# Memory products of a segmented attention in three PSUM banks instead of two

## The chip, the core and the metric

The kernel runs on one core of a Trainium2 chip. The metric is device time in microseconds for one execution; the figure of a kernel is the median of its runs. The profile shows one execution, instruction by instruction, on the core's engines: TensorE (PE, with its weight loads as PEld), VectorE (DVE), ScalarE (ACT), GpSimd (POOL) and the queue that issues most DMAs (SP).

## What is computed

Two independent results stand side by side in the output. One is a Fourier mixing of `B_x` by dense products. The other is a segmented attention over 2048 rows in four segments of 512, with 32 heads of 18 features, in which each segment also reads a memory of the segments before it:

```python
for s in range(N):
    qs, ks, vs = q[:, :, s], k[:, :, s], v[:, :, s]
    logits = jnp.einsum("bhqd,bhkd->bhqk", qs, ks) * scale + mask
    p = _softmax(logits, axis=-1)
    a_dot = jnp.einsum("bhqk,bhkd->bhqd", p, vs)
    pq = phi(qs)
    num = jnp.einsum("bhld,bhde->bhle", pq, M)
    den = jnp.einsum("bhld,bhd->bhl", pq, z)[..., None] + 1e-6
    a_mem = num / den
    o = g * a_mem + (1.0 - g) * a_dot
    outs.append(o)
    pk = phi(ks)
    M = M + jnp.einsum("bhld,bhle->bhde", pk, vs)
    z = z + jnp.einsum("bhld->bhd", pk)
```

The change concerns `num` and `den`, the products of `pq` with the memory.

## The kernel before

**Stages.** The first 220 us project q, k and v, build the memory and read it, segment by segment (loop at L495). The rest interleaves attention with the dense products of the Fourier part, by a list of steps with fixed weights, and ends with the output projection. The order on each engine is the order in which the program is written (manual schedule, L45); nothing is reordered. `later(n, ...)` puts a call n ticks later in that order.

**A segment.** After the nine q and k projections (`project_qk`, from L258) comes the memory stage: four blocks of 128 rows, `project_v(s, j, ...)` (L304), called blocks 0 to 3 here. In a block TensorE makes the two halves of v, 16 heads each, v0 and v1, with 14 matmuls of 288 columns each (L82). ACT copies each half out of PSUM as bf16 (L319) and, in segments 0 to 2, as fp32r (L59); DVE subtracts that copy from it (L60) and writes the remainder `vr` (L322), which is the last read of the PSUM tile. After v0, segments 0 to 2 transpose k (`k_natural`, tiles `kt`, L300), and ACT and DVE make phi of k from it (L214 to L218, POOL L219). After each half the next part of `lookup` runs (L325). From block 1 on, segments 0 to 2 end a block with `accumulate` for the block before (L358), which adds to the memory sums in three further PSUM tiles. In segment 3, DVE has the splitting of the Fourier weights (L122 to L125) and of the first chunks (L451, L453) in its queue instead. SP's queue holds the loads, the copies between DRAM tensors and, among them, the store of each lookup's result `am`.

**A lookup** (L385 to L414; segments 1 to 3, so 12 in all) multiplies pq by the memory. The features lie in five chunks of 128, 128, 128, 128 and 64 rows, with 7, 7, 7, 7 and 4 heads of their own; a window of 8 heads of 19 columns (18 features and z) is taken for each chunk, and the eighth head is shared with the next chunk. Everything is in two parts, high and low, of fp32r: `pq_hi`, `pq_lo`, `md[:, c, 0]` and `md[:, c, 1]`, and of the four products low times low is left out.

- The first half, before v1: chunks one to three, three matmuls of 152 columns each, added up in one PSUM tile `o` (L388 to L391); ACT copies 21 heads into `nd` (L392).
- The second half, after v1: chunk four in a second tile `u`, `pq_hi` against both halves of the memory in one matmul of 304 columns, which leaves two results side by side, and `pq_lo` against the high half (152); chunk five with one matmul of 152 columns for both halves of 4 heads (L397 to L399). ACT copies (L400, L401); DVE adds what is shared or lies beside it (L402 to L405), adds 1e-6, takes the reciprocal and multiplies by the gate (L408 to L410); POOL multiplies (L412), and the result is stored.

The sums in `den` are held in the second tile's last 32 columns, so that this tile is free only after w (L410).

**PSUM.** v0, v1, kt, the q and k projections and the lookup's tiles share a ring of five tiles of one bank each, tag "acc" (`bufs=5`). A new tile waits for the last reader of the tile whose bank it gets. TensorE executes in order, so that a matmul that waits for a bank holds up all that follows it.

Of the kernel before, what the change touches and what calls it, by code (L numbers as in the profile page):

```python
# [12 lines left out]
F32 = mybir.dt.float32  # L13
# [3 lines left out]
AF = mybir.ActivationFunctionType  # L17
OP = mybir.AluOpType
# [4 lines left out]
S, D, H, DH, NSEG, L = 2048, 576, 32, 18, 4, 512  # L23
P = 128
# [16 lines left out]
def infini_attention_and_fnet(ctx: ExitStack, tc: tile.TileContext, xT, wqk, w8, wv, wo, beta, xtT, cT, hT, out):  # L41
    nc = tc.nc
    act, dve, pool, pe = nc.scalar, nc.vector, nc.gpsimd, nc.tensor
# [42 lines left out]
    def later(n, fn, *a):  # L86
        due.setdefault(clock[0] + n, []).append((fn, a))
# [10 lines left out]
    ps = p1.enter_context(tc.tile_pool(name="ps1", bufs=2, space=PSUM))  # L98
# [93 lines left out]
    pq_hi = sb.tile([P, 5, L], F32R, name="pq_hi")  # L192

    pq_lo = sb.tile([P, 4, L], F32R, name="pq_lo")
# [13 lines left out]
    md = sb.tile([P, 5, 2, 8, 19], F32R, name="md")  # L208
# [152 lines left out]
    def memory():  # L361
# [20 lines left out]
            dve.tensor_tensor(md[:64, 4, 1], mf[:64, 4], md[:64, 4, 0].bitcast(F32), OP.subtract)  # L382
        later(4, cut)

    def lookup(s, j):  # L385
        js = slice(j * P, (j + 1) * P)
        nd = sb.tile([P, H, 19], F32, name="nd", bufs=2)
        o = ps.tile([P, 3, 8, 19], F32, name="look", tag="acc", bufs=5)  # L388
        for c in range(3):
            for n, (a, half) in enumerate(((pq_hi, 1), (pq_hi, 0), (pq_lo, 0))):  # L390
                pe.matmul(o[:, c], a[:, c, js], md[:, c, half], start=c + n == 0, stop=True, skip_group_check=True)  # L391
        act.activation(nd[:, :21].rearrange("p (c h) e -> p c h e", c=3), o[:, :, :7], AF.Copy)  # L392
        yield

        u = ps.tile([P, L], F32, name="look", tag="acc", bufs=5)
        u3, u4 = (u[:, at:at + 2 * n].rearrange("p (k h e) -> p k h e", k=2, e=19) for at, n in ((0, 152), (304, 76)))
        pe.matmul(u3, pq_hi[:, 3, js], md[:, 3], start=True, stop=True, skip_group_check=True)  # L397
        pe.matmul(u3[:, 0], pq_lo[:, 3, js], md[:, 3, 0], start=False, stop=True, skip_group_check=True)
        pe.matmul(u4, pq_hi[:, 4, js], md[:, 4, :, 4:], start=False, stop=True, skip_group_check=True)  # L399
        act.activation(nd[:, 21:28], u3[:, 0, :7], AF.Copy)  # L400
        act.activation(nd[:, 28:], u4[:, 0], AF.Copy)  # L401
        dve.tensor_tensor(nd[:, 7:22:7], nd[:, 7:22:7], o[:, :, 7], OP.add)  # L402
        dve.tensor_tensor(nd[:, 28:], nd[:, 28:], u4[:, 1], OP.add)
        dve.tensor_tensor(nd[:, 28], nd[:, 28], u3[:, 0, 7], OP.add)
        dve.tensor_tensor(nd[:, 21:29], nd[:, 21:29], u3[:, 1], OP.add)  # L405
        w = sb.tile([P, H, 1], F32, name="w", bufs=2)
        den = u[:, 456:456 + H, None]
        dve.tensor_scalar(den, nd[:, :, DH:], 1e-6, None, op0=OP.add)  # L408
        dve.reciprocal(den, den)
        dve.tensor_tensor(w, den, g[:, :, None], OP.mult)  # L410
        am = sb.tile([P, H, DH], F32, name="am", tag="p", bufs=5)
        pool.tensor_tensor(am, nd[:, :, :DH], w.to_broadcast([P, H, DH]), OP.mult)  # L412
        later(1, dma, amd[s][j], am.rearrange("p h d -> p (h d)"))
        yield  # L414
# [16 lines left out]
    def c_load(n):  # L431
        if n < len(CHUNKS) and n not in c_seen:
            c_seen.add(n)
            src, at, k = CHUNKS[n]
            t = sr.tile([P, 5, P], F32, name="craw", bufs=4)
            dma(t[:, :k], src[at])
            c_raw[n] = t
# [57 lines left out]
    for s in range(NSEG):  # L495
# [32 lines left out]
        for j in range(4):  # L528
            project_v(s, j, lookup(s, j) if s else iter(()))
            tick()  # L530
            for k in ((0, 1), (2, 3), (4,), ())[j] if s == 0 else ():
                load_x(1, k)
            if more and j in (1, 2):
                split_x(s + 1, j - 1)
            if not more and j == 1:
                stacks(sr, 1)
            if not more and j == 2:
                attention_constants()
            if not more and j == 0:
                h_split(0, 2)  # L540
                h_split(0, 3)
            if not more and j == 1:
                h_split(0, 4)
                c_cut(0, dve)
                c_cut(1, dve)
            if not more and j in (1, 3):
                c_load(3 + j // 2)
            if more and j:
                accumulate(j - 1)
# [4 lines left out]
    ps = ctx.enter_context(tc.tile_pool(name="ps2", bufs=2, space=PSUM, reuse_waits="tile"))  # L554
# [49 lines left out]
    def chunk(n):  # L604
        c_load(n + 4)
        return c_split.pop(n)
# [393 lines left out]
    for t in range(NT):  # L1000
# [3 lines left out]
        for h in range(2):  # L1004
            cs = slice(h * 288, h * 288 + 288)
            o = ps.tile([P, 288], F32, name="d", bufs=3)
# [53 lines left out]
```

## Time and profile before

| | us |
|---|---|
| runs | 999.23, 999.67, 1004.48 |
| median | 999.67 |
| profiled execution | 1000.37 |
| its span, from the first to the last instruction | 998.6 |
| mean granted TensorE clock | 0.999 |

The profile's page gives each engine's busy time and its share of the span, and the chain of work that ended last, followed back from the last instruction. In a timeline each row is the start in us, the duration, the engine, the line of the code, the operation, its output and inputs with their shapes, how many instructions are merged into the row (x2), and in brackets how long the engine was idle before it and what released it. [...] In a table by stretch, each row is a stretch of the span with its length and the busy time of each engine.

### The profile page before, as it was taken

The numbers are of one execution on the slowest core, as the hardware profiler recorded it, in microseconds if no ns is written. First come the engines' busy times: TensorE is split into PE (matmuls) and PEld (weight loads), VectorE is DVE, ScalarE is ACT, GpSimd is POOL, SyncE is SP. The second block draws the span as 40 slices with busy tenths as digits, with TensorE's granted clock in tenths as the row PEclk, the third lists the DMA queues.
The fourth block names the chain that finished last, engine by engine and source line by source line (L and its number), as shares of the span: only waits on it lengthen the run. The fifth ranks groups of instructions, "written<-read, shape, count | busy, mean of one in ns | idle before, by whom it ended". The sixth has DMA issues, their size and how long they took to land.

```text
span 998.6 us, 25575 instructions
## 1 busy us (share of the span) xinstructions
PE 989.0 (99%) x9291; PEld 923.7 (93%) x9291; DVE 753.9 (75%) x2048; ACT 710.9 (71%) x1677; POOL 635.5 (64%) x700
## 2 busy tenths in 40 slices
PE   9999999999999999999999999999999999999998
PEld 7988989898999999999999999999999999999998
DVE  6657668594678777878898888898888899998321
ACT  6667576663887877878788788877767777777243
POOL 2657576686767667666766777776767767767000
PEclk9999999999999999999999999999999999999999
DMA  7447556787578898899999887789999999899555
GB/s 254 161 131 231 205 177 238 236 306 214 138 169 204 208 230 210 209 229 217 254 228 247 220 208 198 181 197 223 223 239 214 242 237 243 228 202 189 137 152 138
DMA packets 305182, 208.92 MB, mean 209 GB/s; under 512 B 206240, under 2 KB 259872, under 8 KB 305056
## 3 DMA queue, kind: packets, MB, share of 16 engines
q1 hardware_dynamic: 304816, 207.15, 80.2%
q8 instruction: 73, 1.20, 0.5%
q14 instruction: 53, 0.43, 0.1%
q10 hardware_dynamic: 240, 0.14, 0.1%
HBM read 121.32 MB, written 57.93 MB: 180 GB/s over the span
## 4 chain that ended last, share of the span: by engine, by line
PE 89%; DVE 3%; DMA 3%; ACT 2%; POOL 2%; issue 1%; SPq 0%; POOLq 0%; DVEq 0%; ACTq 0%
PE d L572 39%; PE s L733 7%; PE d L82 6%; PE v L82 6%; PE pv L851 4%; PE qk L245 4%; PE qk L82 3%; PE d L617 3%; PE d L618 3%; PE d L619 3%; PE pv L852 2%; PE m L358 1%; PE t L807 1%; PE look L391 1%; PE t L810 1%
## 5 line engine op out<-in xcount | busy, mean ns | idle before, releaser
L739 DVE CUSTOM_DVE_ANT_0 s<-s,causal 128x128 f32<-128x128 f32 (+3 forms) x512 | 249.8, 498 | 101.1 <-PE s L733 92.0
L451 POOL TENSOR_TENSOR clo<-craw,chi 128x512 fp32r<-128x512 f32 x158 | 215.9, 1366 | 96.6 <-ACT chi L446 68.0
L572 PE MATMUL d<-wide,chi 128*128 128x288 f32 x1408 | 266.2, 306 | 0.4 <-DVE y L642 0.4
L572 PEld LDWEIGHTS d<-wide,chi 128*128 128x128 f32 x1408 | 211.8, 189 | 2.4 <-DVE y L642 0.6
L572 PE MATMUL d<-wide,clo 128*128 128x288 f32 x704 | 177.6, 319 | 0.0
L773 POOL TENSOR_TENSOR hl<-pf,hl 128x768 f16<-128x768 f32 x64 | 112.7, 1761 | 69.8 <-ACT hl L769 53.9
L733 PE MATMUL s<-ks,qs 108*128 108x128 bf16 (+3 forms) x512 | 133.7, 304 | 1.9 <-DVE negm L739 1.7
L819 ACT ACTIVATE phi<-t 128x384 f16<-128x384 f32 x128 | 61.7, 482 | 103.2 <-PE t L816 103.0
L762 ACT ACTIVATE pf<-s,nb 128x128 f32<-128x128 f32 (+3 forms) x256 | 128.1, 526 | 6.2
L834 DVE TENSOR_TENSOR plo<-pf,phi 128x384 f16<-128x384 f32 (+1 forms) x128 | 126.8, 991 | 0.0
L572 PE MATMUL d<-ab,chi 128*128 128x288 f32 x640 | 126.0, 306 | 0.0
L572 PEld LDWEIGHTS d<-wide,clo 128*128 128x128 f32 x704 | 118.6, 189 | 1.6
L446 ACT ACTIVATE chi<-craw 128x512 fp32r<-128x512 f32 x160 | 100.2, 627 | 5.8 <-DMA craw<-xtT 2.5
L820 ACT ACTIVATE pf<-t 128x384 f32<-128x384 f32 (+1 forms) x192 | 99.5, 518 | 6.2 <-PE t L807 6.0
L572 PEld LDWEIGHTS d<-ab,chi 128*128 128x128 f32 x640 | 98.5, 189 | 0.6
L769 ACT ACTIVATE hl<-pf 128x768 f16<-128x768 f32 (+1 forms) x128 | 87.4, 730 | 2.0
L572 PE MATMUL d<-ab,clo 128*128 128x288 f32 x320 | 84.8, 314 | 0.0
L617 PE MATMUL d<-wide,chi 128*128 128x288 f32 x256 | 84.0, 328 | 0.0
L619 PE MATMUL d<-wide,clo 128*128 128x288 f32 x256 | 75.6, 295 | 0.0
L618 PE MATMUL d<-wide,chi 128*128 128x288 f32 x256 | 75.6, 295 | 0.0
L773 DVE TENSOR_TENSOR hl<-pf,hl 128x512 f16<-128x512 f32 x64 | 67.6, 1056 | 0.1
L834 POOL TENSOR_TENSOR plo<-pf,phi 128x384 f16<-128x384 f32 x64 | 59.4, 928 | 13.0 <-ACT pf L820 10.4
(203 smaller groups left out, 2497.9 us busy)
## 6 DMA issues: line engine op xcount, KB each, us to landing
craw<-cT SPq DMA_DIRECT2D x128, 256.0 KB
ks<-kd SPq DMA_DIRECT2D x32, 432.0 KB
qs<-qd SPq DMA_DIRECT2D x32, 432.0 KB
craw<-xtT SPq DMA_DIRECT2D x32, 320.0 KB
vd<-vs SPq DMA_DIRECT2D x16, 440.0 KB
vst<-vd SPq DMA_DIRECT2D x32, 220.0 KB
qd<-p SPq DMA_DIRECT2D x16, 384.0 KB
kd<-p SPq DMA_DIRECT2D x16, 384.0 KB
```

The source lines that it names most:

```text
L82: pe.matmul(o, a, b, start=n == 0, stop=n == len(terms) - 1)
L446: act.activation(hi, raw[:, :4], AF.Copy)
L451: engine.tensor_tensor(lo, raw[:, :4], hi.bitcast(F32), OP.subtract)
L572: pe.matmul(o[h], a, b[:, h * 288:h * 288 + 288], start=start, stop=stop)
L617: pe.matmul(o, xh[:, k], wl[k][:, cs], start=k == 0, stop=False)
L618: pe.matmul(o, xh[:, k], wh[k][:, cs], start=False, stop=False)
L619: pe.matmul(o, xl[:, k], wh[k][:, cs], start=False, stop=False)
L733: pe.matmul(o[:, c:c + w], q[:, i * P:w], k[:, :w], start=True, stop=True)
L739: dve.tensor_tensor_reduce(o[:, c:c + w], o[:, c:c + w], CAUSAL[0][:, L - w:], scale=scale, scalar=-LOWEST, op0=OP.add, op1=OP.min, accum_ ...
L762: act.activation(f[:, FIRST_COL[i]:FIRST_COL[i] + w], o[:, c:c + w], AF.Exp, bias=nb[:, i:i + 1], scale=-1.0)
L773: engine.tensor_tensor(hl[:, 1, a:b], f[:, a:b], hl[:, 0, a:b], OP.subtract)
L834: (pool if kind == 2 else dve).tensor_tensor(lo[:, a:b], f[:, a:b], hi[:, a:b], OP.subtract)
```

## The change

Each lookup takes three PSUM tiles instead of two. Chunks one, two and three each get a tile and are multiplied as chunk four was: `pq_hi` against both memory halves in one matmul of 304 columns, then `pq_lo` against the high half. Chunk four goes back to three matmuls of 152 columns, which write into the free columns of chunk two's tile; chunk five uses those of chunk three's. Chunks one and two are made before v1, with their ACT copies and the first two adds; chunks four, three and five after v1. The third tile holds `den`. ACT makes five copies per lookup where it made three, and DVE eight adds where it made four; TensorE has 10 matmuls where it had 12.

```diff
     def lookup(s, j):
         js = slice(j * P, (j + 1) * P)
         nd = sb.tile([P, H, 19], F32, name="nd", bufs=2)
-        o = ps.tile([P, 3, 8, 19], F32, name="look", tag="acc", bufs=5)
-        for c in range(3):
-            for n, (a, half) in enumerate(((pq_hi, 1), (pq_hi, 0), (pq_lo, 0))):
-                pe.matmul(o[:, c], a[:, c, js], md[:, c, half], start=c + n == 0, stop=True, skip_group_check=True)
-        act.activation(nd[:, :21].rearrange("p (c h) e -> p c h e", c=3), o[:, :, :7], AF.Copy)
+        u = []
+
+        def views(o):
+            return o[:, :304].rearrange("p (k h e) -> p k h e", k=2, e=19), o[:, 304:456].rearrange("p (h e) -> p h e", e=19)
+
+        def chunk(c):
+            o = ps.tile([P, L], F32, name="look", tag="acc", bufs=5)
+            two, one = views(o)
+            u.append((o, two, one))
+            pe.matmul(two, pq_hi[:, c, js], md[:, c], start=True, stop=True, skip_group_check=True)
+            pe.matmul(two[:, 0], pq_lo[:, c, js], md[:, c, 0], start=False, stop=True, skip_group_check=True)
+
+        def keep(c):
+            two = u[c][1]
+            act.activation(nd[:, 7 * c:7 * c + 7], two[:, 0, :7], AF.Copy)
+
+        def add(c):
+            two = u[c][1]
+            if c:
+                dve.tensor_tensor(nd[:, 7 * c], nd[:, 7 * c], u[c - 1][1][:, 0, 7], OP.add)
+                dve.tensor_tensor(nd[:, 7 * c - 7:7 * c + 1], nd[:, 7 * c - 7:7 * c + 1], u[c - 1][1][:, 1], OP.add)
+
+        chunk(0)
+        keep(0)
+        chunk(1)
+        keep(1)
+        add(1)
         yield
-
-        u = ps.tile([P, L], F32, name="look", tag="acc", bufs=5)
-        u3, u4 = (u[:, at:at + 2 * n].rearrange("p (k h e) -> p k h e", k=2, e=19) for at, n in ((0, 152), (304, 76)))
-        pe.matmul(u3, pq_hi[:, 3, js], md[:, 3], start=True, stop=True, skip_group_check=True)
-        pe.matmul(u3[:, 0], pq_lo[:, 3, js], md[:, 3, 0], start=False, stop=True, skip_group_check=True)
+        one = u[1][2]
+        for n, (a, half) in enumerate(((pq_hi, 1), (pq_hi, 0), (pq_lo, 0))):
+            pe.matmul(one, a[:, 3, js], md[:, 3, half], start=False, stop=True, skip_group_check=True)
+        act.activation(nd[:, 21:28], one[:, :7], AF.Copy)
+        chunk(2)
+        o = u[2][0]
+        u4 = u[2][2].rearrange("p (k h) e -> p k h e", k=2)
         pe.matmul(u4, pq_hi[:, 4, js], md[:, 4, :, 4:], start=False, stop=True, skip_group_check=True)
-        act.activation(nd[:, 21:28], u3[:, 0, :7], AF.Copy)
+        keep(2)
         act.activation(nd[:, 28:], u4[:, 0], AF.Copy)
-        dve.tensor_tensor(nd[:, 7:22:7], nd[:, 7:22:7], o[:, :, 7], OP.add)
+        add(2)
         dve.tensor_tensor(nd[:, 28:], nd[:, 28:], u4[:, 1], OP.add)
-        dve.tensor_tensor(nd[:, 28], nd[:, 28], u3[:, 0, 7], OP.add)
-        dve.tensor_tensor(nd[:, 21:29], nd[:, 21:29], u3[:, 1], OP.add)
+        dve.tensor_tensor(nd[:, 28], nd[:, 28], one[:, 7], OP.add)
+        dve.tensor_tensor(nd[:, 21], nd[:, 21], u[2][1][:, 0, 7], OP.add)
+        dve.tensor_tensor(nd[:, 14:22], nd[:, 14:22], u[2][1][:, 1], OP.add)
+        u = u[2][0]
         w = sb.tile([P, H, 1], F32, name="w", bufs=2)
         den = u[:, 456:456 + H, None]
```

What follows `den` is unchanged, and so is everything outside `lookup`. In the changed program's own numbering the lines behind `lookup` stand 28 lines lower; the prediction names lines by the numbers before the change.

## The prediction
> **What bounds the kernel now.** First the page: busy time, and the chain that ended last.
>
> ```profile
> span 998.6 us, 25575 instructions
> PE 989.0 (99%) x9291; PEld 923.7 (93%) x9291; DVE 753.9 (75%) x2048; ACT 710.9 (71%) x1677; POOL 635.5 (64%) x700
> PE 89%; DVE 3%; DMA 3%; ACT 2%; POOL 2%; issue 1%; SPq 0%; POOLq 0%; DVEq 0%; ACTq 0%
> ```
>
> TensorE is never free, so the test for any edit is whether it shortens or interrupts PE's stream. Then the busy time by stretch, around the lookups: blocks 1 to 3 of segments 1 and 2, and the part of segment 3 in which VectorE works off its backlog.
>
> ```profile
> core 0: us, PE busy (x) PEld busy (x) DVE busy (x) ACT busy (x) POOL busy (x), PEclk, DMA share, GB/s
> 92.34:113.00 20.66, 20.66 (x171) 20.66 (x171) 16.15 (x47) 14.59 (x41) 14.71 (x12) 1.00 0.82 289
> 149.07:169.70 20.63, 20.63 (x171) 20.63 (x170) 16.14 (x47) 14.55 (x40) 14.72 (x12) 1.00 0.78 281
> 205.34:224.84 19.50, 18.98 (x148) 18.70 (x147) 18.65 (x45) 11.56 (x30) 14.78 (x15) 1.00 0.92 333
> ```
>
> In segments 1 and 2 PE is the bound (20.66 of 20.66) and DVE has a fifth of its time free; segment 2 repeats segment 1 within 0.03 us, at a granted clock of 1.00. In segment 3 DVE is full too: 18.65 of 19.50.
>
> **PE work: 12 matmuls a lookup become 10.** Both versions stream 1976 columns (13 x 152, before; 3 x 304 + 7 x 152, after). The PE timeline of block 2, segment 1:
>
> ```profile
> 99.18 0.50 PE L82 MATMUL v<-wide,xh 128*128 128x288 f32 x2
> ...
> 101.56 0.43 PE L391 MATMUL look<-md,pq_hi 128*128 128x152 f32 x2
> ...
> 102.61 0.47 PE L82 MATMUL v<-wide,xh 128*128 128x288 f32 x2
> ...
> 104.52 0.30 PE L397 MATMUL look<-md,pq_hi 128*128 128x304 f32 x1
> 104.66 0.23 PE L398 MATMUL look<-md,pq_lo 128*128 128x152 f32 x1
> 104.72 0.28 PE L399 MATMUL look<-md,pq_hi 128*128 128x152 f32 x1
> 104.84 0.89 PE L358 MATMUL m<-vn,knh 128*128 128x304 f32 x6
> ...
> 106.05 0.50 PE L82 MATMUL v<-wide,xh 128*128 128x288 f32 x2
> ```
>
> Nine 152-column matmuls take 102.61 - 101.56 = 1.05 us, 0.117 each with the hand-over. The three of the second half take 104.84 - 104.52 = 0.32 although one has 304 columns: 0.107 each. So here the number of matmuls counts, not their columns. [...]
>
> New first half: 4 matmuls, 0.14 + 0.07 + 0.14 + 0.07 = 0.42 (0.63 less). New second half: chunk four 3 x 0.11, then 304 + 152 + 152 as now, 0.65 (0.33 more). By itself that is 0.30 us less per lookup, 3.6 in twelve.
>
> **PSUM: the third bank makes PE wait.** In segments 1 and 2 a block takes, from the ring of five "acc" banks, v0, kt, kt, look, v1, look: six tiles; now seven: v0, kt, kt, chunk one, chunk two, v1, chunk three. A tile takes the bank of the fifth before it, so v1 moves from a bank of the block before to the bank of its own v0, and as built its first matmul now waits for L322, the last DVE read of v0. Chunk two takes the bank that the block before frees with w (L410), which v1 waited for until now. Behind the waiting matmul stands all of PE. The DVE timeline from the tail of block 1 to v0 of block 2:
>
> ```profile
> 99.33 0.20 DVE L402 TENSOR_TENSOR nd<-nd,look 128x57 f32<-128x57 f32 x1
> 99.46 0.23 DVE L403 TENSOR_TENSOR nd<-nd,look 128x76 f32<-128x76 f32 x1
> 99.72 0.17 DVE L404 TENSOR_TENSOR nd<-nd,look 128x19 f32<-128x19 f32 x1
> 99.92 0.31 DVE L405 TENSOR_TENSOR nd<-nd,look 128x152 f32<-128x152 f32 x1
> 100.27 0.22 DVE L408 TENSOR_SCALAR look<-nd 128x32 f32<-128x32 f32 x1
> ...
> 100.92 0.19 DVE L410 TENSOR_TENSOR w<-look,g 128x32 f32<-128x32 f32 x1
> 101.03 0.68 DVE L60 TENSOR_TENSOR xl<-raw,xh 128x512 fp32r<-128x512 f32 x1
> 102.04 0.46 DVE L60 TENSOR_TENSOR vn<-v,vn 128x288 fp32r<-128x288 f32 x1 [0.33 <-ACT vn L59]
> 102.42 0.45 DVE L322 TENSOR_TENSOR vr<-v,vs 128x288 f32<-128x288 f32 x1
> ```
>
> L322 ends at 102.87, 3.69 us after v0 began (99.18); v1 now begins at 102.61, 3.43 after. So v1 starts at 3.69 + 0.05 = 3.74: the 0.63 saved in the first half is gone, and 0.31 more. With 0.33 in the second half: **+0.64 us a block**, where DVE is free in time. L322 can't come earlier, as L60 ahead of it waits for ACT's copy of v0, not for DVE.
>
> **DVE: four more adds a lookup.** Steps between starts, from the fence: a 76-element add 0.26, a 19-element add 0.20, a 152-element add 0.35 when the next instruction needs it; 0.12 where a short one is not waited for. The old tail L402 to L408 takes 0.94. The new one is 19, 152, 76, 19, 19, 152: 0.20 + 0.23 + 0.26 + 0.12 + 0.20 + 0.35 = 1.36, taking 0.23 for a 152 that isn't waited for (its 0.31 less the 0.08 by which the starts of L60 and L322, 0.38 apart, overlap 0.46). So w comes 0.44 later (rounded up from 0.42), and the first-half pair (19, 152) adds 0.44 behind L218: 0.88 a lookup. ACT's copies go from three to five, 0.38 more beside 6 us free in the windows row; they cost nothing while the copy of chunk two ends before chunk four is due, 1.9 us of v1 later. If that cover fails, what is late is PE, by ACT's lag.
>
> **Blocks 0 and 1 of segments 1 and 2.** Here DVE is behind. The timeline of all engines:
>
> ```profile
> 90.11 0.47 PE L82 MATMUL v<-wide,xh 128*128 128x288 f32 x2
> 90.25 0.45 DVE L322 TENSOR_TENSOR vr<-v,vs 128x288 f32<-128x288 f32 x1
> ...
> 92.34 0.47 PE L82 MATMUL v<-wide,xh 128*128 128x288 f32 x2
> ...
> 93.34 0.45 DVE L322 TENSOR_TENSOR vr<-v,vs 128x288 f32<-128x288 f32 x1
> 93.71 0.20 DVE L402 TENSOR_TENSOR nd<-nd,look 128x57 f32<-128x57 f32 x1
> ...
> 95.30 0.19 DVE L410 TENSOR_TENSOR w<-look,g 128x32 f32<-128x32 f32 x1
> 95.41 0.45 DVE L60 TENSOR_TENSOR vn<-v,vn 128x288 fp32r<-128x288 f32 x1
> ...
> 95.74 0.47 PE L82 MATMUL v<-wide,xh 128*128 128x288 f32 x2
> 95.77 0.45 DVE L322 TENSOR_TENSOR vr<-v,vs 128x288 f32<-128x288 f32 x1
> ```
>
> Block 0: v1 waits for L322, 90.25 + 0.45 + 0.05 = 90.75, not 90.11: +0.64; with the second half +0.97. Block 1: L322 of v1 moves to 93.98, the tail starts at 94.35, w at 94.35 + 1.59 + 0.44 = 96.38; behind it in DVE's queue L60 at 96.49 and L322 at 96.85, ending at 97.30. v1 starts at 97.35, not 95.74: +1.61, and with its second half +1.94 for both blocks. Blocks 2 and 3 add 0.64 each (DVE is just free: w of block 1 at 102.97, xl until 103.76, L60 due at 102.04 + 1.94 = 103.98). A segment costs 1.94 + 1.28 = 3.22; two, **6.44**.
>
> **Segment 3** has no kt and no memory sums: the ring returns to v0 for v0, so there PE waits for DVE only as far as DVE lags, and DVE is full. It then hands over to attention:
>
> ```profile
> 207.77 3.39 DVE L122 TENSOR_TENSOR wide<-raw,wide 128x576 fp32r<-128x576 f32 x2
> ...
> 224.71 0.19 DVE L410 TENSOR_TENSOR w<-look,g 128x32 f32<-128x32 f32 x1
> 224.84 0.70 DVE L739 CUSTOM_DVE_ANT_0 s<-s,causal 128x512 f32<-128x512 f32 x1
> ...
> 225.65 0.27 PE L733 MATMUL s<-ks,qs 108*128 108x256 bf16 x1 [1.32 <-DVE negm L739]
> ```
>
> Four lookups put 4 x 0.88 = **3.52** us in front of L739, on which PE already waits (1.32): 225.65 becomes 229.17. PE can't be the later one: its own waits for v0's bank and for the bank of chunk two lie inside the same DVE queue. Unknown is L122: two take 3.39 here beside POOL, and 1.13 is the low end of one in the row below, so pushing them out of or into POOL's work may move 3.39 - 2.26 = 1.1 either way.
>
> ```profile
> 202.46 1.13 DVE L122 TENSOR_TENSOR wide<-raw,wide 128x576 fp32r<-128x576 f32 x1
> ...
> 242.56 0.23 PE L790 MATMUL trm<-ident,mb 128*128 128x128 bf16 x1 [0.68 <-POOL mb L786]
> ```
>
> After that PE waits little (0.68 here), so almost nothing can be given back. SP's issue order is unchanged; its waits for am move with w, by the same 0.4 to 3.5.
>
> **Sum.** 6.44 + 3.52 = 9.96 on the profiled execution's 1000.37 us (span 998.6, 1.8 around it): 1010.3. That run stood 0.7 above the median 999.67, so against the median 1009.6. Bounds: 1.0 for columns against matmuls, 1.1 for L122, 0 to 0.7 returned at the 0.68 wait, 0.05 to 0.15 per new wait (0.8 in eight): 1006.0 to 1012.5.
>
> **Rivals.**
> - *The waits are hidden, the saved matmuls count* (not slower). If DVE read v0 before v1 is due, twelve lookups save 0.30: 999.67 - 3.6 = 996.1. It decides the other way once L322 ends more than 2.80 us after v0's start (3.43 - 0.63); the row says 3.69. For it: only DVE's 75%. Chance 0.05.
> - *Only segment 3's backlog is paid*: v1 gets another bank, segments 1 and 2 save 8 x 0.30, 3.52 is paid: 1000.8. Against it: the built wait names L322. Chance 0.07.
> - *Only the ring is paid*: DVE regains its 3.52 in segment 3 because L122 runs faster apart from POOL, and four lookups save 1.2: 999.67 + 6.44 - 1.2 = 1004.9. For it: 3.39 against 2.26. Chance 0.10.
> - *DVE lags in every block, not only block 1*: block 1 costs 0.97, blocks 2 and 3 as much if L60 is late by 0.33 more: + 4 x 0.33, and POOL slows L122 by 1.1: 1012.0; with each new wait at 0.15, 1013. For it: DVE is free only 0.2 us before L60 is due. Chance 0.10.
> - That the change doesn't do what it says is excluded: as built, 120 lookup matmuls stand for 144.
>
> **How the numbers follow.** Forecast 1009.6, chance 0.68. A measurement of this kernel tells 0.5% (5.0 us) from no change. Range 1004.5 to 1013.0: the forecast's bounds and the two rivals beside them. Faster by over 0.5% needs less than 994.7: 0.02, the far end of the first rival. Within 0.5%: the rest of it, the second rival and a little of the third, 0.12. Slower: 0.86.
>
> **What would show it.** In the changed profile: PE waits for DVE vr L322 ahead of v in segments 1 and 2, 0.9 us in blocks 2 and 3; chunk two waits for w in block 1 (0.7); L739 begins about 10 us later than 224.84; the memory stage's 20.66 from v0 of block 1 to the next segment grows to 22.9. It is wrong if PE shows no wait for L322, if L322 comes earlier than 3.6 us after v0's start, or if segment 3 grows by less than 2 us.

## The result, and the profile after

| | before | after |
|---|---|---|
| median of 5 runs, us | 1000.29 (999.23 to 1004.48) | 1011.64 (1009.76 to 1013.32) |
| profiled execution, us | 1000.37 | 1009.85 |
| its span, us | 998.6 | 1008.1 |
| mean granted TensorE clock | 0.999 | 1.000 |

The changed kernel takes 1.0104 times as long (95% interval 1.0087 to 1.0122): it is slower by about 11 us. Of its five runs, the two at a mean granted clock of 0.997 took 1012.40 and 1013.32 us, the three at 1.000 took 1009.76 to 1011.64. All line numbers from here on are those of the changed program; lines behind `lookup` stand 28 higher than in the prediction, and the lookup's own are L399 and L400 (a chunk against both halves), L409 and L410 (the two adds of `add`), L420 (chunk four), L425 (chunk five) and L438 (w).

The changed kernel's page, span and busy time:

```profile
span 1008.1 us, 25619 instructions
...
PE 989.9 (98%) x9267; PEld 921.8 (91%) x9267; DVE 762.3 (76%) x2096; ACT 712.6 (71%) x1701; POOL 635.6 (63%) x700
```

TensorE has 24 matmuls less and is as long busy as before (989.0), in a span that is 9.5 us longer. The time was lost while PE stood still. What it stood for is in the view of its waits (in total, times, longest):

```profile
PE v L82 <- DVE vr L322: 5.3, 10, 0.7
...
PE look L399 <- DVE r L271: 1.4, 3, 0.5
PE d L645 <- DVE nd L431: 1.4, 1, 1.4
PE look L399 <- DVE w L438: 1.1, 2, 0.6
...
PE s L761 <- DVE negm L767: 0.4, 2, 0.2
```

In the kernel before, the wait for negm was the only one of the attention's start, and no v waited for vr:

```profile
PE s L733 <- DVE negm L739: 1.7, 3, 1.3
```

Now ten do: eight in segments 1 and 2, one for each block, and two in segment 3. The 1.3 us at negm has become 1.4 at the second tile `d` of the product stage, which gets the bank of the last lookup's chunk two. (The last add that reads this bank is L430; the view names L431, the add behind it.)

Blocks 1 to 3 of segment 1 in PE's timeline, cut to the lookups and the first matmuls of v:

```profile
93.00 0.46 PE L82 MATMUL v<-wide,xh 128*128 128x288 f32 x2
...
96.34 0.38 PE L399 MATMUL look<-md,pq_hi 128*128 128x304 f32 x1 [0.54 <-DVE w L438]
...
97.07 0.50 PE L82 MATMUL v<-wide,xh 128*128 128x288 f32 x2 [0.28 <-DVE vr L322]
...
100.88 0.50 PE L82 MATMUL v<-wide,xh 128*128 128x288 f32 x2
...
103.26 0.39 PE L399 MATMUL look<-md,pq_hi 128*128 128x304 f32 x1
103.48 0.23 PE L400 MATMUL look<-md,pq_lo 128*128 128x152 f32 x1
103.56 0.34 PE L399 MATMUL look<-md,pq_hi 128*128 128x304 f32 x1
103.74 0.23 PE L400 MATMUL look<-md,pq_lo 128*128 128x152 f32 x1
104.71 0.50 PE L82 MATMUL v<-wide,xh 128*128 128x288 f32 x2 [0.74 <-DVE vr L322]
...
106.65 0.35 PE L420 MATMUL look<-md,pq_hi 128*128 128x152 f32 x2
106.83 0.27 PE L420 MATMUL look<-md,pq_lo 128*128 128x152 f32 x1
106.94 0.35 PE L399 MATMUL look<-md,pq_hi 128*128 128x304 f32 x1
107.13 0.23 PE L400 MATMUL look<-md,pq_lo 128*128 128x152 f32 x1
107.19 0.28 PE L425 MATMUL look<-md,pq_hi 128*128 128x152 f32 x1
107.31 0.89 PE L358 MATMUL m<-vn,knh 128*128 128x304 f32 x6
...
108.52 0.50 PE L82 MATMUL v<-wide,xh 128*128 128x288 f32 x2
```

The rows overlap: the matmul of 103.26 lasts 0.39, and the next begins 0.22 after it. What an instruction takes is counted here from start to start.

And what v1 of block 2 waits for, in DVE's timeline, with the copy by ACT in front of it:

```profile
103.31 0.40 ACT L59 ACTIVATE vn<-v 128x288 fp32r<-128x288 f32 x1
103.74 0.46 DVE L60 TENSOR_TENSOR vn<-v,vn 128x288 fp32r<-128x288 f32 x1 [0.27 <-PE look L400]
104.12 0.45 DVE L322 TENSOR_TENSOR vr<-v,vs 128x288 f32<-128x288 f32 x1
```

The reader sees PE finish the first half of the lookup early (103.74 is its last matmul) and then stand until v0's own bank is read. L60 has to wait for ACT's copy, which it subtracts and which ends at 103.71; the bracket names the lookup's L400, which ends at the same moment and which L60 doesn't read. L322 ends at 104.57, 3.69 us after v0 began at 100.88, as it did before; v1 begins 0.14 later. The block takes 108.52 - 100.88 = 7.64 where it took 6.87.

For comparing kernels, the span is cut by PE's own starts: segments 1 and 2 from the first matmul of v to the next segment's first `qk`; segment 3 from its first v to the fourth group of `s` matmuls (231.57 in the kernel before); and the rest, from there to the end of the span. The table leaves out the q and k projections between the segments (29.95 to 29.97 us each, 30.14 or 30.15 in the two kernels with six banks) and the first 85 to 86 us, which only the kernels with six banks change; the profiled execution of before was the latest there (86.12, the others 84.80 to 85.70) and stood 1.3 us above the median of the runs beside the first four experiments (999.10).

| us, one profiled execution each | segment 1 | segment 2 | segment 3 | the rest |
|---|---|---|---|---|
| before | 26.79 | 26.77 | 31.96 | 767.03 |
| after | 30.49 (+3.70) | 30.46 (+3.69) | 34.68 (+2.72) | 766.89 (-0.14) |

All of it lies in the three stages that read the memory.

### The profile page after: what moved, and what is told of

The parts are those of the page before. It is cut to its first block, busy times and chain, and to the rows that moved or that the text cites. A ratio compares the mean times of both kernels' runs of the same rounds, so it can differ in the third digit from the quotient of the medians.

```text
span 1008.1 us, 25619 instructions
## 1 busy us (share of the span) xinstructions
PE 989.9 (98%) x9267; PEld 921.8 (91%) x9267; DVE 762.3 (76%) x2096; ACT 712.6 (71%) x1701; POOL 635.6 (63%) x700
## 4 chain that ended last, share of the span: by engine, by line
PE 85%; DVE 5%; ACT 4%; DMA 2%; issue 2%; POOL 1%; SPq 0%; DVEq 0%; POOLq 0%; ACTq 0%
PE d L600 39%; PE s L761 7%; PE d L82 6%; PE v L82 4%; PE pv L879 4%; PE d L645 3%; PE d L646 3%; PE d L647 3%; PE qk L245 3%; PE pv L880 2%; PE qk L82 2%; PE t L835 1%; PE m L358 1%; DMA kd<-kd 1%; PE t L838 1%
```

## The experiments

The theory on trial: in segments 1 and 2 the price is PE's wait for v0's own bank, which the third tile brings into the ring; in segment 3 it is DVE's four more adds, in front of the first attention tile. The rivals: the adds cost everywhere, or chunk four's return to three passes does. The experiments ran in two groups beside runs of the kernel before (medians 999.10 and 999.85).

| | us, median | ratio to before (95%) | segment 1 | segment 2 | segment 3 | rest |
|---|---|---|---|---|---|---|
| new_seg12 | 1007.68 | 1.0085 (1.0070 to 1.0100) | +3.71 | +3.71 | +0.20 | +0.93 |
| new_seg3 | 1001.77 | 1.0030 (1.0019 to 1.0041) | +0.02 | 0.00 | +2.49 | -0.40 |
| one_ahead | 1004.94 | 1.0057 (1.0042 to 1.0072) | +0.97 | +0.94 | +2.75 | +0.11 |
| no_adds | 1008.81 | 1.0086 (1.0068 to 1.0105) | +3.44 | +3.42 | +0.89 | +1.65 |
| six_banks | 1006.99 | 1.0074 (1.0059 to 1.0089) | +0.95 | +1.01 | +5.06 | -0.40 |
| before_six | 1004.66 | 1.0049 (1.0034 to 1.0064) | +0.20 | +0.22 | +3.22 | -0.68 |
| mix | 1003.58 | 1.0044 (1.0027 to 1.0060) | +0.96 | +0.95 | +0.24 | +0.66 |

The stages are differences to the profiled execution of before, in us. The rest swings by -0.7 to +1.7, though no edit reaches into it; what moves it was not tried.

**The change in segments 1 and 2 alone, and in segment 3 alone.** Both lookups are kept, as `lookup_two` (before) and `lookup_three` (after):

```diff
-            project_v(s, j, lookup(s, j) if s else iter(()))
+            project_v(s, j, (lookup_three if s in (1, 2) else lookup_two)(s, j) if s else iter(()))
```

and with `s in (3,)` for the other.

> The new lookup in segments 1 and 2, the old one in segment 3. Theory (in segments 1 and 2 the price is PE's wait for the bank of v0, in segment 3 it is VectorE's four more adds a lookup): the two segments keep what they cost in the changed kernel's trace, 3.7 us each, and segment 3 costs nothing: 7.4 us over the kernel before. Rival (the adds are the price, wherever they stand, 12 alike): two thirds of the 11.4 us between the medians, 7.6, which can't be told from it here; the waits in the trace tell them apart: by the theory PE waits for vr in blocks 2 and 3 as in the changed kernel, 0.74 us each.

> The old lookup in segments 1 and 2, the new one in segment 3. Theory: only VectorE's backlog before the first attention tile is paid, 2.4 us in the changed kernel's trace (four times 0.88 less what the L122 pair gives back): 2.4 over the kernel before. Rival (all of the price is the bank of v0): segment 3 has no such wait and PE has fewer matmuls there, 4 x 0.30 = 1.2 us faster than before. Second rival (adds alone, all alike): 3.8 over.

Measured: 8.6 and 2.7 us over before by the medians (7.4 and 2.4 were expected; the trace of the first has 0.9 in the rest), together 11.3, the 11.35 of the whole change. So the two prices are separate and add up. PE's waits in new_seg12:

```profile
PE v L82 <- DVE vr L322: 4.2, 8, 0.7
```

Eight waits, one for each block that has the new lookup with `kt` beside it.

**Chunk two made behind v1.** The same work, the same adds and the same number of banks; only v1 comes ahead of chunk two, so that v1 no longer gets v0's bank:

```diff
-        chunk(1)
-        keep(1)
-        add(1)
         yield
+        chunk(1)
         one = u[1][2]
...
+        keep(1)
         act.activation(nd[:, 21:28], one[:, :7], AF.Copy)
...
+        add(1)
         add(2)
```

> The changed kernel with chunk two moved behind v1, so that v1 again takes the bank that the block before frees with w; the work of every engine is that of the changed kernel. Theory: no wait for vr ahead of v1; blocks 2 and 3 take 0.26 us less than before the change, block 0 0.54 more (its v1 waits for r as before), block 1 0.7 more (w comes later by eight adds in one tail), so 0.75 a segment, and segment 3 keeps its 2.4: 4 us over the kernel before, 7 under the changed one. Rival (the adds are the price): the adds are all there, so 11 over the kernel before. Rival (the three passes of chunk four are the price): they are all there too, 11 over.

Measured: 5.8 over before where 4 was expected. Half of the 11.35 is gone, though every matmul, copy and add of the change is there, the three passes of chunk four too: in segments 1 and 2 the price falls from 3.70 to 0.97 and 0.94. (The two adds of chunk two's first half now stand behind v1 as well; the next experiment takes adds away and leaves the order.) PE's waits:

```profile
PE v L82 <- DVE vr L322: 2.0, 3, 0.8
PE d L645 <- DVE nd L431: 1.7, 1, 1.7
PE v L82 <- ACT ke L214: 1.5, 2, 0.7
...
PE v L82 <- DVE r L271: 1.4, 3, 0.5
```

The three waits for vr that are left are those of v0 in segment 3. What remains of the price in segments 1 and 2 are waits of v1 in blocks 0 and 1. In block 0 it gets a bank of the q and k projections (r L271, 0.50). In block 1 (0.73) the view names ke L214, ACT's reading of `kt`, which ends at 95.36; but counted through the ring v1's bank is that of the third lookup tile of block 0, whose last reader, w (L438), ends at 95.35, and v1 begins at 95.50. So it is w, as expected. Block by block: +0.57 and +0.74 in blocks 0 and 1 (expected 0.54 and 0.7), -0.18 and -0.16 in blocks 2 and 3 (expected -0.26). Blocks 2 and 3 of segment 1, in which PE waits for nothing, begin and end with these rows of its timeline:

```profile
99.54 0.51 PE L82 MATMUL v<-wide,xh 128*128 128x288 f32 x2
...
106.23 0.50 PE L82 MATMUL v<-wide,xh 128*128 128x288 f32 x2
...
112.93 0.47 PE L245 MATMUL qk<-xh,wide 128*128 128x512 f32 x1
```

They take 6.69 and 6.70 us, 0.17 less than the 6.87 and 6.86 of before. That is what the saved matmuls are worth when nothing stands in their way. Of the 1.8 us more than expected, 0.8 lies in the three stages (4.66 where 3.9 was expected). Where the other 1.0 lies isn't shown: between the profiled executions the whole difference is only 3.7 (1004.11 against 1000.37); this kernel's stood 0.8 below its median, that of before 1.3 above the one beside it.

**The four adds taken out.** The two lines under `if c:` in `add` are removed, so four of the eight adds of a lookup are left out; the banks and PE's work stay:

```diff
             two = u[c - 1][1]
-            if c:
-                dve.tensor_tensor(nd[:, 7 * c], nd[:, 7 * c], u[c - 1][1][:, 0, 7], OP.add)
-                dve.tensor_tensor(nd[:, 7 * c - 7:7 * c + 1], nd[:, 7 * c - 7:7 * c + 1], u[c - 1][1][:, 1], OP.add)
```

> The changed kernel with four of its eight adds per lookup left out (those of chunks one and two into the next chunk, both halves), so that VectorE has four adds as before the change. Theory: the bank of v0 is still waited for, 0.74 us in blocks 2 and 3, because ahead of its last read stands ACT's copy and not VectorE's adds; block 1 loses its wait for w; segment 3 goes back to the kernel before or 1 us under it. Sum: 2 x (1.1 + 0.4 + 0.77 + 0.77) - 0.5 = 5.5 over the kernel before. Rival (the adds are the price everywhere): without them nothing is left of it, and the saved matmuls count: 0 to 3 under the kernel before.

Measured: 9.7 over before where 5.5 was expected, a miss. Segments 1 and 2 keep 3.44 and 3.42 of their 3.70 and 3.69, so the adds are worth only 0.26 and 0.27 there; expected was 3.0 each. PE's waits:

```profile
PE v L82 <- DVE vr L322: 4.5, 8, 0.7
PE look L417 <- ACT nd L404: 1.9, 2, 1.5
```

All eight waits for v0's bank are still there without the adds, so the rival that the adds cost in every stage falls. In segment 3 the price goes from 2.72 to 0.89, so most of it goes with the adds; but it was expected to go to nothing or below, and 1.0 of what went is the pair of L122, which takes 2.39 here where it took 3.39 before the change (last section). A wait that was 0.3 in the changed kernel has grown to 1.9: chunk four (L417) waits for ACT's copy of chunk two, and in ACT's queue the copy of v ahead of it waits for a DMA that still reads its `vs` buffer:

```profile
226.93 0.42 ACT L319 ACTIVATE vs<-v 128x288 bf16<-128x288 f32 x1 [3.91 <-DMA vd<-vs]
```

The rest of this execution is 1.65 longer, the largest of all; why is open.

**A sixth bank for the ring, in the changed kernel and in the one before.** The memory sums are put into two PSUM tiles, which frees a bank; `tag="acc"` gets six everywhere:

```diff
-SUMS = ((0, 0, True), (1, 0, True), (2, 0, True), (0, 2, False), (1, 2, True))
+SUMS = ((0, 0, True), (0, 2, False), (1, 0, False), (1, 1, False), (1, 2, True))
...
-    m_ps = [ps.tile([P, 3, 8, 19], F32, name=f"m{b}", bufs=1) for b in range(3)]
+    m_ps = [ps.tile([P, 3, 8, 19], F32, name=f"m{b}", bufs=1) for b in range(2)]
```

The sums now take two matmuls more for each `accumulate`, in both kernels.

> The changed kernel with six banks in the ring instead of five: the memory sums are packed into two banks, for which two of their chunks add both value halves in one place, 13 matmuls instead of 11 per accumulation. Theory: with a sixth bank v1 no longer takes the bank of its own v0, and segments 1 and 2 cost about 0.3 us each over the kernel before (0.33 a block in the second half, mostly returned in the first), plus 0.8 in each of segments 0, 1 and 2 for the sums (4 accumulations x 2 matmuls x 0.1); segment 3 keeps up to 2.7: about 5.7 over the kernel before, 3.3 over the kernel before with the same six banks. Rival (the adds or the three passes of chunk four are the price): 11 over the kernel before with the same six banks.

> The kernel before with the same six banks and packed sums, as the measure for the run with six banks. All theories: 12 accumulations x 2 matmuls x 0.1 = 2.4 us over the kernel before, if its waits for banks were hidden as the trace says.

Measured: 7.1 over before where 5.7 was expected (six_banks). The sixth bank takes segments 1 and 2 of the changed kernel from +3.70 to +0.95 and +1.01, and 0.2 of that is the sums' own (before_six); what is left, 0.8 each, is more than the 0.3 expected and lies in blocks 0 and 1, where v1 waits for r and w (0.5 each). So once v1 isn't given v0's bank, by another order or by another bank, the price there falls to less than 1 us in both ways. But before_six was a miss: 4.8 over before where 2.4 was expected. The view of its waits, in its own numbering, says where:

```profile
PE d L617 <- DVE vr L322: 3.2, 1, 3.2
```

The larger number of matmuls costs little: 0.2 a segment, and 0.17 to 0.19 more in the projections behind it. But in segment 3 the first `d` tile of the next stage now gets the bank of the last v, which DVE reads only behind its backlog. With five banks that tile had one of the three banks of the memory sums. In six_banks the same wait is 2.5, and chunk four waits 2.0 for ACT's copy where it waited 0.3 with five banks:

```profile
PE d L645 <- DVE vr L322: 2.5, 1, 2.5
PE look L420 <- ACT nd L404: 2.0, 2, 1.8
```

Nor is the wait all that is paid at `d`. Behind it the granted clock falls to half. By stretch (the clock is the third figure from the end), before_six ahead of the wait, which ends at 223.83, and behind it:

```profile
214.00:220.00 6.00, 6.00 (x49) 6.00 (x48) 5.74 (x14) 3.82 (x11) 4.86 (x4) 1.00 1.05 407
225.00:227.80 2.80, 2.80 (x14) 2.80 (x13) 1.14 (x4) 0.78 (x2) 2.18 (x2) 0.50 0.16 65
```

From the first `d` matmul to the second group of `s` 4.30 us pass (223.83 to 228.13) where the kernel before took 2.86 (220.01 to 222.87), so about 1.4 of the 3.22 in segment 3 go with the lower clock, in which the 288-column matmuls begin 0.24 apart where they begin 0.13 apart in the kernel before; in six_banks, with 4.29, it is the same 1.4.

By the medians the change costs 2.3 us with six banks (1006.99 against 1004.66); by the three stages it is 3.4, about the 3.3 that was expected, but by luck: segments 1 and 2 give 0.75 and 0.79 where 0.3 was expected, and segment 3 gives 1.84 where 2.7 was.

**The best of both.** Chunk two behind v1 in segments 1 and 2, the lookup of before in segment 3:

> In segments 1 and 2 the changed lookup with chunk two behind v1, in segment 3 the old lookup. Theory: what the earlier run with chunk two behind v1 left in segments 1 and 2, 0.95 us each by its trace, and nothing in segment 3: 2 us over the kernel before. Rival (the adds are the price): two thirds of 11.3, 7.5 over.

Measured: 3.7 over before where 2 was expected. The stages give 0.96, 0.95 and 0.24, as expected; 0.66 is in the rest, and between the profiled executions the whole difference is 1.9, so that the medians' other 1.8 has no place in a trace. No version beats the kernel before: even without the wait for v0's bank, the 0.17 us that the lookup's fewer matmuls save in an undisturbed block is less than the waits that a third tile brings to the others.

## Why the prediction was right

Forecast 1009.6 (9.96 more), measured 1011.64 (11.35 more by the medians, 9.48 between the profiled executions). Sign, place and mechanism held; that the sum came so near is luck, as two of its terms erred by 0.95 and 0.80 in opposite directions.

- **Matmuls: 0.30 saved a lookup.** The second half was right (forecast 0.65; 107.31 - 106.65 = 0.66). The first half was too cheap: forecast 0.42, and it takes 103.26 to about 103.81, where the fifth matmul would have begun: 0.55. The 304-column matmuls take 0.22 and 0.18 here, and not the 0.14 that the old second half showed for one. So a lookup of these blocks saves 0.16, which one_ahead's undisturbed blocks confirm (0.17). (In segment 3 a first half takes 0.45, with 0.13 and 0.18.) It cost the forecast nothing, as v1 stands waiting behind it. The 1.0 that the forecast's bounds set aside for columns against matmuls is shown by no run; what the changed trace shows is 0.13 to 0.26 us from the start of a 304-column matmul to the next start, with only four of 36 below 0.17.
- **The ring: +0.64 a block.** Shown by one_ahead and six_banks. The row that the forecast read, L322 ending 3.69 after v0's start, is the same to the hundredth after the change. Counted from 103.81, where PE could have gone on, v1 is 0.90 late, the 0.9 of the forecast. Mis-sized was what lies between L322's end and v1's start: taken as 0.05, measured 0.14. With 0.04 more in the second half, blocks 2 and 3 cost 0.77 and 0.78 and not 0.64.
- **Blocks 0 and 1: 1.94.** Measured 1.11 + 1.04 = 2.15, by the same two terms. The wait of chunk two for w in block 1 (forecast 0.7) is there, 0.54. Not forecast was chunk two's wait in block 0 for a projection's bank (r L271, 0.49); v1 would have stood there anyway. A segment costs 3.70 and not 3.22, two cost 7.39 and not 6.44.
- **DVE, +0.44 on the tail and +0.44 in front.** As a delay of DVE's own queue it holds: the tail from L409 to w takes 1.99 (100.70 to 102.69) where L402 to w took 1.59, so +0.40, and the pair in front takes 0.43 (231.50 to 231.93). As a price in segments 1 and 2 it is 0.26 and 0.27 (no_adds).
- **Segment 3: 3.52.** Measured 2.72. The step that was mis-sized is the unknown that the forecast had bounded by 1.1: the two L122 gave back 0.83 of it, as the last section shows, so that little more than three of the four lookups are paid. From the first v to the reduction that answers to L739, DVE takes 27.88 (206.53 to 234.41, the next fence) where it took 25.23 (199.61 to 224.84): 2.65 more. That the reduction is 9.57 later in all, where about 10 was forecast, is again the sum of the two errors. And PE does not wait for the reduction's result, as was forecast, but earlier, for chunk two's bank at `d` (1.37); that too is freed by the DVE queue.
- **Nothing given back later.** Right: the rest is 766.89 after 767.03. The wait of 0.68 became 0.3, inside that.
- **The rivals.** That the waits are hidden, and that only segment 3 or only the ring is paid, are excluded by new_seg12 and new_seg3. That DVE lags in every block doesn't hold either: in blocks 2 and 3 L60 begins 2.86 after v0, as before.

DVE's timeline at the end of segment 3, with the row that answers to L739 of before:

```profile
234.28 0.19 DVE L438 TENSOR_TENSOR w<-look,g 128x32 f32<-128x32 f32 x1
234.41 0.70 DVE L767 CUSTOM_DVE_ANT_0 s<-s,causal 128x512 f32<-128x512 f32 x1
```

The two errors, 0.95 too little in segments 1 and 2 and 0.80 too much in segment 3, nearly cancel. Against the medians 1.4 us is missing, for which no row of a kept trace shows a mechanism: the profiled execution of after stands 1.8 below the median of its five runs, that of before 0.1 above.

## What to carry to other kernels

A tile added to a ring of PSUM banks moves every later tile to another bank: count the ring through, stage by stage and across the border into the next stage, and look for a tile that gets the bank of its own predecessor, and, at the border, for one that gets a bank read behind a backlog (the sixth bank cost 3.2 us there). Such a wait doesn't depend on how much work was saved in front of it, because PE only reaches it sooner (L322 ended 3.69 us after v0's start before the change and after). Where the ring can't grow, changing the order of two tiles takes the wait away at no cost in work (3.70 to 0.97 a segment here).

## What the runs showed of the hardware

**L122 on DVE beside POOL.** The forecast read 1.13 us as the price of one L122 (128x576) and the 3.39 of two as a slowing beside POOL. But the first four L122 of this size take 0.74 to 0.76, so 1.13 was not the low end, and taken singly the rows end some 0.6 us behind POOL's. POOL's timeline before the change, and DVE's:

```profile
207.74 1.17 POOL L283 TENSOR_TENSOR p<-r,p 128x512 bf16<-128x512 f32 x1
208.87 1.68 POOL L412 TENSOR_TENSOR am<-nd,w 128x576 f32<-128x576 f32 x1
```

```profile
207.77 1.75 DVE L122 TENSOR_TENSOR wide<-raw,wide 128x576 fp32r<-128x576 f32 x1
...
209.45 1.72 DVE L122 TENSOR_TENSOR wide<-raw,wide 128x576 fp32r<-128x576 f32 x1
```

POOL's and DVE's after the change:

```profile
214.86 1.17 POOL L283 TENSOR_TENSOR p<-r,p 128x512 bf16<-128x512 f32 x1
215.99 1.69 POOL L440 TENSOR_TENSOR am<-nd,w 128x576 f32<-128x576 f32 x1
```

```profile
215.73 0.91 DVE L122 TENSOR_TENSOR wide<-raw,wide 128x576 fp32r<-128x576 f32 x1
...
216.57 1.72 DVE L122 TENSOR_TENSOR wide<-raw,wide 128x576 fp32r<-128x576 f32 x1
```

Each L122 ends 0.61 to 0.62 us after the end of the POOL instruction beside it, whenever it began: 209.52 against 208.91, 211.17 against 210.55, 216.64 against 216.03, 218.29 against 217.68. In the changed kernel DVE comes to the first L122 later, when less of L283 is left, and gets back 1.75 - 0.91 = 0.84 of the 0.88 that the first lookup's adds had taken. The same happens in new_seg3, one_ahead and six_banks (pairs of 2.56 to 2.57), and not in new_seg12, before_six and mix (3.39 to 3.40), which have the old lookup there. In no_adds DVE comes first, by 0.01, and the order is turned round:

```profile
213.92 0.75 DVE L122 TENSOR_TENSOR wide<-raw,wide 128x576 fp32r<-128x576 f32 x1
```

```profile
213.93 1.77 POOL L283 TENSOR_TENSOR p<-r,p 128x512 bf16<-128x512 f32 x1
```

Now L122 takes 0.75, as the first four of the program do (0.74 to 0.76), and POOL's L283 takes 0.60 more than its 1.17. No run was made for this, so it rests on these rows; what holds the one engine up beside the other is not shown.

**From a DVE result to the waiting matmul** 0.14 or 0.15 us pass in all eight blocks of segments 1 and 2 (104.57 to 104.71 in block 2). It isn't always so: the two v of segment 3 begin 0.05 and 0.06 behind the end of L322 (212.92 to 212.97, 218.65 to 218.71), and the matmul behind negm before the change 0.06 (225.59 to 225.65). What makes the difference was not tried.

**The clock behind a long wait.** Behind the waits of 3.19 us (before_six) and 2.46 us (six_banks) at `d` the granted clock was 0.50 for some 3 us, and the 288-column matmuls began 0.24 apart where they begin 0.13 apart at 1.00. Behind shorter waits at the same place, up to 1.69 us (one_ahead), it stayed at 1.00. No other wait of PE in segments 1 to 3 is longer than 1.81 us. Whether the wait is the cause was not tried.
